# One soft-MoE kernel on one core: the first pair folded before it is turned, three expert matrices in other homes, and a new order of all steps

## The chip, the cores and the metric

One NeuronCore of a Trainium2 chip runs the whole program. The metric is device microseconds (us) of one execution; a lower time is better. TensorE does the matrix products and turns (transposes), VectorE and ScalarE the elementwise work and the copies out of PSUM, GpSimd a few elementwise steps, and SyncE (SP in the profile) issues every DMA from one queue, in order.

## The reference

The input x is (8, 2496, 256). It is transformed by a Fourier transform along the sequence and along the features, and the real part goes through a soft mixture of 8 experts with 4 slots each. Only the parts that matter:

```python
X = np.fft.fft(np.fft.fft(x, axis=1), axis=2).real     # 8 x 2496 x 256
x = X.reshape(19968, 256)
logits = x @ phi                                       # 19968 x 32
d = softmax over the tokens (axis 0) of logits
slot_input = d.T @ x                                   # 32 x 256
for e in range(8):                                     # 4 slots per expert
    h = np.maximum(slot_input[e] @ w1[e], 0.0)         # 256 -> 1024
    slot_out[e] = h @ w2[e]                            # 1024 -> 256
c = softmax over the slots (axis 1) of logits
return c @ slot_out                                    # 19968 x 256
```

The softmax over the tokens needs the maximum and the sum over all tokens, so no expert can start before all of x has been worked on, and no output before the experts are done.

## The kernel before, in words

The batch is worked on as four pairs (0 to 3). The 2496 tokens of a sequence are factored as 64 x 39, and each pair is loaded as five tiles `x{p}{t}` of 1 MB (tile 0 has 896 KB). A step is one short name in the string `PLAN`; the loop at the end of `_build` walks through it and issues each step's instructions to its engines. The order is written out by hand in this string: every engine gets its instructions in exactly this order, and waits only where it needs a result, a buffer or a transfer. `X020` loads half 0 of tile 2 of pair 0; `=x02:R0` says that the tile lives in home R0 from here on. A home is a fixed buffer: six R homes of 8 KB per partition, eighteen E homes of 4 KB, ten M, four D, two X homes, and eight B homes, the PSUM banks. A step that gives a home to a new tile waits until all readers of the old one are done. A suffix `/a` or `/v` says which engine copies, ScalarE or VectorE.

For each pair the steps are these. `F` adds a tile's rows to their mirror rows (VectorE, line 344), `G` and `H` add and subtract the halves of the feature axis and write the folded tile `e{p}{t}` into an E home (VectorE, line 355). `T` turns a folded tile on TensorE (line 360, four turns for each half), `A` copies the turned half out of PSUM, `Zo` and `Ze` multiply it by the folded phi (line 385), `Y`, `t`, `y`, `a`, `b`, `l`, `L`, `M` and `N` finish the logits. `R`, `V`, `v`, `vb`, `W` and `w` find the maxima, `E` takes exponentials, `q`, `e`, `f`, `d` and `D` bring them back to token order, and `u` multiplies them with the folded tiles `e{p}{t}` (line 595). An E home that held `e{p}{t}` is therefore free only after `u{p}{t}`. `sel`, `mm`, `mr`, `mx`, `me`, `ac`, `acT` (line 644), `at`, `si` and `sT` combine the pairs into the inputs of the slots.

Not all pairs go this way. In the kernel before, three tiles of pair 0 (0, 1 and 4) are turned raw: `TT` (line 370) turns the unfolded tile as soon as it has landed, adding the mirror row in PSUM, and `Zr` (line 417) folds the feature halves inside the product. The tiles are folded by `F`, `G` and `H` all the same, later, for step `u`. Pair 3 is loaded a second time, already turned (`XT`, `FT`, `Zt`), in both kernels.

The experts: w1 comes as eight matrices of 1 MB (`I0` to `I7`, tiles `w10` to `w17`, R homes), w2 as sixteen of 512 KB (`J0` to `J15`, E homes). `h` multiplies the slots by w1 (line 683), `r` is the ReLU on ScalarE, `x` a turn on VectorE, `s0j` and `s1j` multiply by w2 for the two halves of the output features (line 701, matrices J0 to J7 and J8 to J15). `so`, `rep` and `rh` spread the result.

The weights over the slots: `O` (line 721) and `Q` turn the logits back, `ca` to `ce` take the softmax over the slots (VectorE, ScalarE and GpSimd), `lT` and `lc` turn it. `po` is the last product (line 784), `ev` copies its four banks to an `o` tile in an R home, `S` stores it (line 796): halves of 512 KB for pair 0, whole tiles of 1 MB for the others. `dm` is a filler: a product of constants, whose result nobody reads (line 266).

Of the kernel before, what the change touches and what calls it, by code (L numbers as in the profile page):

```python
# [49 lines left out]
l00=bl00:B0,bm00:B2 y12/a=zt1:M4 F01 F12 H12=e12:E3 G12 X22=x22:R0 F22 H22=e22:E8 A110/a=et100:E9 A111/a  # L50
Zo10=bz10:B6 A100/a L010/a=lt0:M5 L011/a L000/a X20=x20:R1 F20 G22 T121=bT121:B1 T120=bT120:B4 Ze10 H20=e20:E4 G20
A121/a A120/a X21=x21:R4 F21 Y10/a Zo11=bz11:B3 Ze11 Y11/a t10=bt10:B5 M01 H21=e21:E5 y10/a T221=bT221:B1 N01
t11=bt11:B4 G21 y11/a T220=bT220:B6 X23=x23:R2 F23 G23=e23:E12 T201=bT201:B3 T200=bT200:B5 A201/a=et201:E10
X24=x24:R3 A220/a=et210:E14 XT34=xt34:R0 F24 H23 A200/a=et200:E9 a12=ba12:B4 b12/a=oo1:M6 a11=ba11:B3 b11/a
a10=ba10:B6 b10/a T211=bT211:B5 A221/a=et211:E17 A211/a T210=bT210:B4 A210/a l10=bl10:B7,bm10:B3 L101/a=lt1:M7
L001/a l11=bl11:B6,bm11:B1 Zo20=bz20:B5 Ze20 L100/a L110/a L111/a T230=bT230:B4 T231=bT231:B2 H24=e24:E16
T241=bT241:B3 Y20/a=zs2:M8 t20=bt20:B1 A231/a A241/a=et221:E10 G24 T240=bT240:B5 R01 V01=bv01:B2 A230/a y20/a=zt2:M9
Zo22=bz22:B3 A240/a=et220:E9 Zo21=bz21:B4 Ze22 Y22/a Ze21 Y21/a M10 M00 v01 FT34 Zt32=bz32:B1 XT33=xt33:R1
t22=bt22:B5 FT33 vb01/a=me01:X0 t21=bt21:B3 Y32/a=zs3:M0 XT32=xt32:R4 FT32 N00 N10 y21/a XT30=xt30:R2 W01
t32=bt32:B4 Zt31=bz31:B1 R00 V00=bv00:B0 y22/a a20=ba20:B3 a21=ba21:B5 y32/a=zt3:M1 w01/a E010=d01:D0 E011 R10  # L60
V10=bv10:B7 v00 Y31/a b20/a=oo2:M3 b21/a FT30 vb00/a=me00:X1 t31=bt31:B4 y31/a XT31=xt31:R3 a22=ba22:B2 W00 FT31
b22/a q011=q01:D1 M11 v10 vb10/a=me10:X0 J4=w24:E10 w00/v N11 q010 Zt30=bz30:B1 C3 l21=bl21:B3,bm21:B5
l20=bl20:B4,bm20:B2 E000=d00:D2 E001 R11 V11=bv11:B0 Y30/v t30=bt30:B6 q000=q00:D3 q001 L211/a=lt2:M2 L210/a M21 v11
vb11/v=me11:X1 W10 L201/a L200/a w10/a H01=e01:E17 M20 N20 C4 X30=x30:R0 J2=w22:E9 J11=w211:E14 X33=x33:R1
e01=be010:B1,be011:B5 y30/a E101=d10:D0 e00=be000:B2,be001:B7 f010/a=es0:M4 W11 w11/v G01 f011/v E100 R20
a30=ba30:B6 O02=bc02:B1 O00=bc00:B4 q101=q10:D2 Q00/v=c0:M6 a32=ba32:B0 a31=ba31:B5 N21 R21 q100 E110=d11:D1 f001/a
X34=x34:R4 X31=x31:R2 X32=x32:R3 f000/a d001=bd001:B7 d000=bd000:B2 b32/a=oo3:M8 b30/a b31/a l31=bl31:B0,bm31:B4
D001/a=ds0:M9 E111 q110=q11:D3 q111 D000/a L311/a=lt3:M3 L310/a l30=bl30:B6,bm30:B3 L300/a M31 N31
e10=be100:B5,be101:B7 L301/a f100/a=es1:M0 e11=be110:B2,be111:B4 M30 V21=bv21:B3 N30 f101/a v21 O20=bc20:B0 R31
Q20/a=c2:M1 vb21/a=me21:X0 f110/a f111/a V20=bv20:B5 v20 d101=bd101:B7 d011=bd011:B6 D011/a d100=bd100:B0  # L70
vb20/a=me20:X1 d010=bd010:B2 D100/a=ds1:M8 Q02/a V31=bv31:B4 I6=w16:R5 W21 D010/a w21/a O32=bc32:B6 E211=d21:D0 R30
W20 V30=bv30:B0 O01=bc01:B1 Q01/a F30 v31 vb31/v=me31:X0 u00=bu0:B2 v30 u01 F33 sel=bsel:B3 mm H33=e33:E7 u02 w20/a
E210 D101/a u03 q210=q21:D1 q211 u04 W31 vb30/a=me30:X1 E200=d20:D2 W30 O22=bc22:B1 O21=bc21:B5 O31=bc31:B3
O30=bc30:B7 U0/v w30/v w31/a E300=d30:D3 F32 mr G33 F34 Q22/a J10=w210:E17 J3=w23:E0 E201 q201=q20:D0 G32=e32:E2
d111=bd111:B2 d110=bd110:B4 Q30/a=c3:M4 D110/a e21=be210:B0,be211:B1 D111/a u10=bu1:B7 u11 u12 mx u13 u14 J5=w25:E11
H32 q200 f210/a=es2:M5 E301 f211/v E311=d31:D1 E310 Q32/a Q21/a me q301=q30:D2 e20=be200:B4,be201:B2 U1/a f200/a
f201/a I2=w12:R1 q300 I1=w11:R3 J6=w26:E13 e30=be300:B0,be301:B1 f301/a=es3:M2 f300/a G30=e30:E1 d211=bd211:B6
q311=q31:D3 q310 H30 e31=be310:B5,be311:B7 F31 ca00 G31=e31:E3 I4=w14:R0 f311/a f310/a d300=bd300:B4 d210=bd210:B2
D210/a=ds2:M0 Q31/a d201=bd201:B1 D300/a=ds3:M3 d301=bd301:B0 D301/a D211/v H31 ca20 d200=bd200:B7 J1=w21:E15 D200/a
# [816 lines left out]
```

## Time and profile before

| | us |
|---|---|
| median of 3 runs (174.19 to 175.49) | 174.72 |
| the profiled execution | 174.32 |
| its span, from the first to the last instruction | 172.5 |
| PE / DVE / ACT / POOL busy | 144.7 / 127.7 / 108.4 / 15.2 |
| moved by DMA | 64.34 MB: read 43.57, written 20.45 |

Times are of the profiled execution and count from the start of its span. What lies around the span is 1.8 us. A busy PE is not a PE at its peak, since the ends of matmuls are modelled and overlap the next one.

### The profile page before, as it was taken

What the parts mean: (1) busy time and instruction counts of PE and PEld (TensorE: products, weight loads), DVE (VectorE), ACT (ScalarE), POOL (GpSimd) and SP (SyncE); (2) the same over time, 40 slices, a digit from 0 to 9 for tenths busy, and PEclk for the clock granted to TensorE, in tenths of its full rate; (3) what the DMA queues carried; (4) which work ended last, traced back from release to release, by engine and by line L of the source; (5) the groups of instructions that cost most, each with busy time, mean ns of one, the idle gap of its engine ahead of it and who ended that gap; (6) DMA issues with size and microseconds to landing.
All of it is one profiled execution on the core that took longest, in us unless ns stands there. A gap on an engine that the chain in (4) does not pass through costs nothing.

```text
span 172.5 us, 5028 instructions
## 1 busy us (share of the span) xinstructions
PE 144.7 (84%) x2080; PEld 100.4 (58%) x2080; DVE 127.7 (74%) x226; ACT 108.4 (63%) x270; POOL 15.2 (9%) x27
## 2 busy tenths in 40 slices
PE   7298799999999999999999999699899988884000
...
DVE  0587979999999999899999789788966563066000
...
PEclk9879999999999999999999999999999999697555
...
GB/s 179 356 410 416 418 417 420 419 421 414 418 424 402 409 423 418 422 70 201 365 368 417 408 408 400 349 281 157 400 390 404 421 409 414 421 421 419 422 418 167
DMA packets 12406, 64.34 MB, mean 373 GB/s; under 512 B 1504, under 2 KB 1888, under 8 KB 7904
## 3 DMA queue, kind: packets, MB, share of 16 engines
...
q8 instruction: 16, 0.26, 0.6%
...
HBM read 43.57 MB, written 20.45 MB: 371 GB/s over the span
## 4 chain that ended last, share of the span: by engine, by line
PE 60%; DMA 19%; ACT 9%; issue 2%; SPq 1%; DVE 1%; ACTq 0%
PE B L784 10%; DMA R<-xh 6%; PE B L595 5%; DMA out<-R 5%; PE B L360 5%; PE B L569 5%; PE B L456 4%; PE B L385 4%; DMA R<-w1h 4%; DMA cs<-c 4%; PE B L701 4%; ACT M L260 4%; ACT R L260 3%; PE B L539 3%; PE B L402 3%; PE B L721 3%
## 5 line engine op out<-in xcount | busy, mean ns | idle before, releaser
L260 ACT COPY M<-B 128x480 f32<-128x480 f32 (+13 forms) x107 | 41.8, 441 | 8.6 <-PE B L385 2.1
L260 ACT COPY R<-B 128x512 f32<-128x512 f32 (+1 forms) x50 | 25.8, 590 | 10.8 <-PE B L784 5.8
L344 DVE TENSOR_TENSOR R<-R 128x1024 f32<-128x1024 f32 (+1 forms) x20 | 23.2, 1165 | 9.2 <-DMA R<-xh 9.1
L258 DVE COPY R<-B 128x512 f32<-128x512 f32 (+1 forms) x30 | 18.8, 664 | 14.4 <-PE B L784 12.2
L260 ACT COPY E<-B 128x512 f32<-128x512 f32 (+1 forms) x34 | 18.7, 596 | 16.0 <-PE B L360 8.0
L784 PE MATMUL B<-E,rh 32*128 32x512 f32 (+2 forms) x192 | 25.3, 577 | 3.6 <-ACT E L260 2.3
L355 DVE TENSOR_TENSOR E<-R 128x512 f32<-128x512 f32 x40 | 26.4, 686 | 0.6
L784 PEld LDWEIGHTS B<-E,rh 32*128 32x128 f32 x192 | 11.8, 200 | 11.2 <-ACT E L260 3.7
L760 POOL TENSOR_TENSOR M<-M,cm 128x640 f32<-128x640 f32 x8 | 10.0, 1263 | 83.9 <-DVE cm L755 83.9
L360 PE MATMUL B<-cs,E 128*128 128x128 f32 x96 | 13.9, 288 | 3.4 <-DVE E L355 3.4
L360 PEld LDWEIGHTS B<-cs,E 128*128 128x128 f32 x96 | 11.4, 147 | 5.0 <-DVE E L355 5.0
L526 ACT ACTIVATE D<-M,nm 124x128 f32<-124x128 f32 x44 | 14.2, 403 | 0.2
L266 PE MATMUL B<-warm 128*128 128x256 f32 x28 | 10.1, 476 | 1.1 <-POOL warm L821 1.1
L456 PE MATMUL B<-cs,M 128*128 128x128 f32 x88 | 10.8, 275 | 0.0
L456 PEld LDWEIGHTS B<-cs,M 128*128 128x128 f32 x88 | 10.4, 192 | 0.0
L569 PE MATMUL B<-M,cs 128*64 128x320 f32 x64 | 9.7, 439 | 0.4 <-issue 0.4
L595 PE MATMUL B<-E,M 128*32 128x129 f32 x320 | 9.5, 274 | 0.0
L385 PE MATMUL B<-E,wphi 128*32 128x256 f32 (+1 forms) x168 | 9.1, 352 | 0.0
L683 PE MATMUL B<-R,sT 128*32 128x512 f32 x64 | 7.7, 597 | 1.6 <-DMA R<-w1h 1.4
L595 PEld LDWEIGHTS B<-E,M 128*32 128x32 f32 x320 | 8.6, 110 | 0.8 <-ACT M L260 0.6
L701 PEld LDWEIGHTS B<-E,E 128*32 128x32 f32 x256 | 6.7, 110 | 3.3 <-issue 1.7
L491 DVE TENSOR_TENSOR M<-B,M 124x320 f32<-124x320 f32 (+1 forms) x16 | 8.0, 514 | 0.4 <-ACT M L260 0.3
(103 smaller groups left out, 199.3 us busy)
## 6 DMA issues: line engine op xcount, KB each, us to landing
...
```

The lines of the kernel that those rows point to most:

```text
L258: v.tensor_copy(dst, src)
L260: sc.copy(dst, src)
L344: v.tensor_tensor(x[:, lo], x[:, lo], x[:, hi], op=ALU.add)
L355: v.tensor_tensor(d, x[:, 0:4, 0:128], x[:, 0:4, 128:256], op=ALU.subtract if k else ALU.add)
L360: pe.transpose(b[:, g * 128 : g * 128 + 128], x[:, g, k * 128 : k * 128 + 128], ident)
L385: pe.matmul(z[32 * g : 32 * g + 32, o : o + n], wphi[:, w, :], turned_x(p, u, k)[:, g].rearrange("p h q a -> p (h q a)"), start=w != 0, st ...
L456: pe.matmul(d[:, i * 128 : i * 128 + 128], z[:, g].rearrange("p h q -> p (h q)"), C("wa"), start=True, stop=True)
L526: sc.activation(d[:, g], L[:, g], AF.Exp, bias=nms[:, p, hf, g : g + 1], scale=1.0)
L569: pe.matmul(b[64 * h : 64 * h + 64, :320], C("wb")[:, 64 * k : 64 * k + 64], s[:, 16 * hf : 16 * hf + 16, h], start=True, stop=True, tile_ ...
L595: pe.matmul(b[32 * g : 32 * g + 32, 0:129], d[:, k, c, :], x[:, c % 4, 0:129] if k == 0 else x[:, c % 4, 127:256], start=cc == 0, stop=cc ...
L701: pe.matmul(b[32 * g : 32 * g + 32], h[:, 4 * (2 * (j % 2) + f) + g, :], w[:, f, g], start=j == 0 and f == 0, stop=j == 7 and f == 1, tile ...
L784: pe.matmul(view(f"bp{p}{b}{i}", 512)[:, q * n : q * n + n], rh[rows, dc], l[rows, :n], start=True, stop=True, tile_position=(32 * i, 0),)
```

## The change

1. All five tiles of pair 0 are folded by VectorE first and then turned (`F`, `G`, `H`, `T`, `Zo`, `Ze`); no `TT` and no `Zr` is left.
2. `w17` comes in two halves of 512 KB in E homes (`I70` in E5, `I71` in E14), and `w214` and `w215` live in R homes (R0 and R3). The functions for it were there.
3. All steps stand in another order, with other homes; some copies change between ScalarE and VectorE. Pair 0's tiles are loaded in the order 3, 2, (pair 1's tile 0), 1, 0, 4 in place of 2, 3, (pair 1's tile 4), 0, 4, 1. The fillers are again fourteen: eight stand ahead of `acT` and six behind, before it was six and eight.
4. The table `wb`, equal to `wa`, is gone (64 KB less in `C2`), and `usb`, `sos` and the fillers' constants share one buffer, `spare`.

The diff, cut:

```diff
 PLAN = """
-dm4=bw4:B0 X021=x02:R0 dm13=bw13:B1 dm9=bw9:B2 dm3=bw3:B3 X020 F02 C0 X031=x03:R1 H02=e02:E0 T021=bT021:B4 G02 X030
-T020=bT020:B5 dm11=bw11:B6 A021/a=et011:E1 C1 F03 P phi=bphi:B7 H03=e03:E2 G03 T031=bT031:B0 X140=x14:R2 X001=x00:R3
-T030=bT030:B1 A020/a=et010:E3 X000 TT000=bT000:B2 wphi wneg A031/v Zo01=bz01:B3 A030/v Ze01 TT001=bT001:B4 X141
-A000/a=et000:E4 Y01/a=zs0:M0 F14 A001/a=et001:E5 H14=e14:E6 t01=bt01:B5 F00 G00=e00:E7 y01/a=zt0:M1 G14
-T141=bT141:B6 X040=x04:R4 X041 TT040=bT040:B7 TT041=bT041:B0 X011=x01:R5 T140=bT140:B1 A041/a=et021:E8 X010
-A040/v=et020:E9 TT010=bT010:B2 A010/a TT011=bT011:B3 A140/a=et120:E10 A011/a F04 H00 X10=x10:R0 Zr02=bz02:B4
-G04=e04:E11 A141/a=et121:E12 Zr00=bz00:B5 Zo12=bz12:B7 Y02/a Y00/a Ze12 Y12/a=zs1:M2 X13=x13:R1 t02=bt02:B0 y02/a
...
-u32 ac1 H34 ca31 cb00/v cb20/v cb01/v u24 U2/v u33 u34 ac2 ac3 dm12=bw12:B4 acT=bac:B0 at k0=bk0:B7 O10=bc10:B1
-si0=bs0:B5 cc20 I3=w13:R4 J9=w29:E4 J0=w20:E5 J8=w28:E1 cc00 sT0/a k2=bk2:B6 k3=bk3:B2 K3/a h100=bh10:B3 cc01 K2/a
-O12=bc12:B4 dm5=bw5:B0 I7=w17:R0 O11=bc11:B5 cd20 cd00 ca30 si1=bs1:B2 sT1/v k1=bk1:B6 K1/a K0/a h000=bh00:B0 h001
-h110=bh11:B2 h010=bh01:B6 h011 tk Q12/a=c1:M5 Q10/a cd01 ce01/g r00=hs00:D0 ca21 x00=hT00:E8 cb30/v I5=w15:R2
-s10=bo1:B7 s00=bo0:B4 s01 Q11/a h111 r01=hs01:D1 x01=hT01:E3 ca10 r11=hs11:D2 J7=w27:E12 h101 r10=hs10:D3 cb31/v
...
+dm1=bw1:B0 dm2=bw2:B1 dm13=bw13:B2 X031=x03:R0 X030 P F03 H03=e03:E0 X021=x02:R1 G03 C0 dm3=bw3:B3 T031=bT031:B4
+dm12=bw12:B5 X020 F02 A031/v=et011:E1 H02=e02:E2 T030=bT030:B6 C1 A030/a=et010:E3 phi=bphi:B7 X10=x10:R2
+T021=bT021:B0 A021/a G02 wphi X010=x01:R3 F10 H10=e10:E4 dm8=bw8:B1 G10 X011 F01 H01=e01:E5 X000=x00:R4
+T020=bT020:B2 Zo01=bz01:B3 A020/a T100=bT100:B5 dm4=bw4:B4 A100/a=et100:E6 Ze01 dm5=bw5:B6 Y01/a=zs0:M0 X001 F00
+H00=e00:E7 T011=bT011:B7 A011/a=et001:E8 t01=bt01:B1 X040=x04:R5 G01 X041 X12=x12:R0 G00 C2 X11=x11:R1 T001=bT001:B0
+T101=bT101:B2 T010=bT010:B4 y01/a=zt0:M1 A001/a F04 H04=e04:E9 X141=x14:R2 A010/a=et000:E10 T000=bT000:B5 A000/a
+Zo00=bz00:B6 G04 Ze00 Y00/a F12 T041=bT041:B3 T040=bT040:B7 H12=e12:E11 A041/a=et021:E12 t00=bt00:B1
+A040/a=et020:E13 y00/a Zo02=bz02:B0 Ze02 Y02/a T121=bT121:B4 wneg t02=bt02:B5 X140 G12 F11 H11=e11:E14
+A121/v=et111:E15 y02/a G11 T120=bT120:B6 a01=ba01:B3 b01/a=oo0:M2 F14 H14=e14:E16 A101/a=et101:E17 a02=ba02:B7 b02/a
+G14 a00=ba00:B1 b00/a T111=bT111:B0 A111/a X13=x13:R3 A120/a=et110:E1 T110=bT110:B5 l01=bl01:B4,bm01:B3
+L011/a=lt0:M3 A110/a L010/a l00=bl00:B2,bm00:B7 Zo10=bz10:B1 Ze10 T141=bT141:B0 T140=bT140:B6 F13 L001/a M01
+H13=e13:E3 Y10/a=zs1:M4 t10=bt10:B5 G13 T131=bT131:B3 A141/a=et121:E8 T130=bT130:B1 Zo12=bz12:B0 y10/a=zt1:M5 A131/a
...
+q201=q20:D0 q200 d010=bd010:B3 L301/a H31 M31 M30 N31 N30 E211=d21:D2 d011=bd011:B1 e20=be200:B4,be201:B7
+d101=bd101:B0 D010/a D011/a D001/a u00=bu0:B3 X32=x32:R0 u01 X34=x34:R1 R30 E110 u02 q111=q11:D3 q110 R31 k0=bk0:B1
+u03 u04 e11=be110:B2,be111:B5 E210 f200/a=es2:M2 f201/a U0/a f110/a F34 V30=bv30:B6 f111/a V31=bv31:B4 v30
+X33=x33:R2 v31 vb30/a=me30:X1 vb31/a=me31:X0 J0=w20:E7 I70=w170:E5 O12=bc12:B7 D101/a=ds1:M7 G34=e34:E2 q211=q21:D0
...
+J1=w21:E10 u30=bu3:B7 u22 u31 cc20 u23 H32=e32:E13 G32 u32 u24 u33 u34 U2/a O30=bc30:B1 Q30/a ca10 ac1 ac2 ac3
+acT=bac:B6 at si0=bs0:B2 k2=bk2:B0 cd20 si1=bs1:B5 sT0/a sT1/v ca30 K2/v ca31 I3=w13:R0 h000=bh00:B3 J11=w211:E9
+h100=bh10:B4 cd00 h001 J9=w29:E12 k3=bk3:B7 ce00/g I6=w16:R4 J6=w26:E17 h010=bh01:B1 h101 h011 cb21/g K3/a tk
+lT00=bl00x:B6 r00=hs00:D1 x00=hT00:E1 s00=bo0:B2 s01 J8=w28:E13 r01=hs01:D3 x01=hT01:E6 J15=w215:R3 J12=w212:E3
+h110=bh11:B5 r10=hs10:D2 x10=hT10:E2 h111 lc00/a=ls00:E7 cb30/g s02 cc30 r11=hs11:D0 s03 cd01 x11=hT11:E10 s04 s05
+ce01/v s06 cd30 cb10/g s07 cc21 so0/a lT01=bl01x:B0 rep0=br0:B7 cc10 rh0/a lc01/a=ls01:E5 ce20/g lT20=bl20x:B3
+po00=bp000:B1,bp001:B4,bp002:B6,bp003:B5 lc20/v=ls20:E14 ev001/v=o00:R2 po20=bp200:B2,bp201:B7,bp202:B0,bp203:B3
+ev000/a ev002/a ev003/v ev203/a=o20:R1 ev201/a s10=bo1:B1 s11 cd21 po02=bp020:B4,bp021:B6,bp022:B5,bp023:B3
...
-            ("wb", np.block([[np.cos(al), np.sin(al)], [-np.sin(al), np.cos(al)]])),
...
-        usb = const("usb", 128, NPAIR - 1, 129)
+
+        spare = const("spare", 128, (NPAIR - 1) * 129)
+        usb = spare.rearrange("p (i n) -> p i n", n=129)
...
-        sos = const("sos", 128, D)
+        sos = spare[:, :D]
...
-        warm = const("warm", 128, max(WARM)) if WARM else None
+        warm = spare[:, : max(WARM)] if WARM else None
...
-                    b[64 * h : 64 * h + 64, :320], C("wb")[:, 64 * k : 64 * k + 64], s[:, 16 * hf : 16 * hf + 16, h],
+                    b[64 * h : 64 * h + 64, :320], C("wa")[:, 64 * k : 64 * k + 64], s[:, 16 * hf : 16 * hf + 16, h],
```

## Rows read from the trace of the kernel before

**Rows 1.** The page's 40 equal slices of the span, and all that was moved.

```profile
PE   7298799999999999999999999699899988884000
DVE  0587979999999999899999789788966563066000
PEclk9879999999999999999999999999999999697555
GB/s 179 356 410 416 418 417 420 419 421 414 418 424 402 409 423 418 422 70 201 365 368 417 408 408 400 349 281 157 400 390 404 421 409 414 421 421 419 422 418 167
DMA packets 12406, 64.34 MB, mean 373 GB/s; under 512 B 1504, under 2 KB 1888, under 8 KB 7904
```

**Rows 2.** Five stretches: busy us of PE, PEld, DVE, ACT, POOL; clock, DMA, GB/s.

```profile
0.00:21.00 21.00, 14.52 (x129) 11.18 (x129) 12.81 (x22) 5.35 (x9) 1.44 (x15) 0.92 0.93 354
21.00:49.00 28.00, 28.00 (x349) 22.29 (x353) 26.39 (x36) 22.57 (x51) 0.24 (x2) 1.00 1.01 418
49.00:98.80 49.80, 49.35 (x955) 37.58 (x954) 48.10 (x92) 42.13 (x131) 0.00 (x0) 1.00 0.91 359
98.80:117.00 18.20, 16.58 (x314) 9.44 (x313) 14.98 (x33) 7.69 (x19) 7.32 (x5) 1.00 0.95 361
117.00:172.50 55.50, 36.29 (x348) 19.90 (x348) 25.41 (x47) 30.61 (x61) 6.20 (x5) 0.84 0.92 374
```

**Rows 3.** Waits of SP, the queue of all DMAs: total us, times, longest.

```profile
SPq L270 <- DVE E L355: 42.0, 18, 4.3
SPq L270 <- PE B L614: 11.8, 1, 11.8
```

**Rows 4.** The chain that ended last: start us, us, what.

```profile
22.97 2.74 PE B L417 x64
25.70 0.66 PE B L385 x24
...
27.16 0.87 PE B L360 x8
...
32.46 1.34 PE B L472 x16
...
103.96 7.09 DMA R<-w1h
...
148.87 8.32 DMA out<-R
```

**Rows 5.** Groups by line and shape: us busy, mean ns, idle before.

```profile
L355 DVE TENSOR_TENSOR E<-R 128x512 f32<-128x512 f32 x40 | 26.4, 686 | 0.6
L344 DVE TENSOR_TENSOR R<-R 128x1024 f32<-128x1024 f32 x16 | 19.4, 1219 | 8.2 <-DMA R<-xh 8.2
```

**Rows 6.** Timeline of PE at the start, and around the experts: start us, us.

```profile
7.94 1.97 PE L360 MATMUL B<-cs,E 128*128 128x128 f32 x8 [3.38 <-DVE E L355]
...
13.71 0.98 PE L370 MATMUL B<-cs,R 128*128 128x128 f32 x7 [1.06 <-DMA R<-xh]
14.63 1.50 PE L385 MATMUL B<-E,wphi 128*32 128x256 f32 x24
...
21.00 1.97 PE L370 MATMUL B<-cs,R 128*128 128x128 f32 x16 [0.89 <-DMA R<-xh]
...
101.31 0.54 PE L721 MATMUL B<-cs,M 124*128 124x124 f32 x3
101.69 0.60 PE L266 MATMUL B<-warm 128*128 128x256 f32 x2
102.12 0.59 PE L721 MATMUL B<-cs,M 124*128 124x124 f32 x4
...
111.09 1.06 PE L683 MATMUL B<-R,sT 128*32 128x512 f32 x8 [1.41 <-DMA R<-w1h]
...
116.91 1.14 PE L784 MATMUL B<-E,rh 32*128 32x512 f32 x8
```

**Rows 7.** Timeline of SP's queue: when the first store is issued.

```profile
119.59 41.71 SPq L796 DMA_DIRECT2D out<-R  x25
```

More of the change, by code (lines that the diff above doesn't have):

```diff
@@ L50 @@
[L50 to L79, printed above, removed]
@@ L85 @@
-s10=bo1:B7 s00=bo0:B4 s01 Q11/a h111 r01=hs01:D1 x01=hT01:E3 ca10 r11=hs11:D2 J7=w27:E12 h101 r10=hs10:D3 cb31/v
-cb21/g ce20/g x11=hT11:E2 x10=hT10:E16 ca11 cb11/v lT20=bl20x:B1 cb10/g cc10 cc30 ce00/g s02 s03 s04 s05
-lc20/v=ls20:E7 s06 s07 lT00=bl00x:B0 cc21 so0/a rep0=br0:B5 lT01=bl01x:B6 rh0/a lc01/a=ls01:E6 cd21 lc00/v=ls00:E1
-po20=bp200:B2,bp201:B3,bp202:B1,bp203:B4 ev203/v=o20:R3 ev200/a ev201/a cc31 cc11 ev202/v s11 s12 J13=w213:E5
-J15=w215:E15 J12=w212:E9 po00=bp000:B5,bp001:B6,bp002:B0,bp003:B2 ev000/a=o00:R5 ev001/a s13 cd10 cd30 s14 ev003/a
@@ new lines @@
+a21=ba21:B7 w00/v L111/a FT32 E001=d00:D0 M11 a22=ba22:B0 v10 N11 a20=ba20:B1 R11 V11=bv11:B3 E011=d01:D1
+vb10/a=me10:X0 W10 Y32/a=zs3:M1 b22/a=oo2:M2 t32=bt32:B5 b21/a b20/a l21=bl21:B6,bm21:B4 XT33=xt33:R5 C4 E000 FT33
+y32/a=zt3:M4 L211/a=lt2:M5 w10/a E010 l20=bl20:B0,bm20:B7 L210/a J7=w27:E15 XT31=xt31:R0 Zt31=bz31:B1 FT31
+q000=q00:D2 XT30=xt30:R1 FT30 Zt30=bz30:B5 v11 q001 M21 N21 vb11/v=me11:X1 e00=be000:B2,be001:B4 R21 V21=bv21:B6
+E100=d10:D3 L200/a L201/a M20 f000/v=es0:M7 N20 W11 Y31/a Y30/a O11=bc11:B7 t30=bt30:B1 E101 y30/a t31=bt31:B5
@@ new lines @@
+J5=w25:E8 O21=bc21:B2 O20=bc20:B0 w11/v O22=bc22:B3 y31/a v21 vb21/a=me21:X0 Q21/a=c2:M9 Q20/a Q11/a=c1:M0
+q011=q01:D0 R20 V20=bv20:B1 v20 vb20/a=me20:X1 q010 X31=x31:R2 q101=q10:D2 F31 q100 E111=d11:D1 a32=ba32:B5
+b32/a=oo3:M2 a31=ba31:B2 b31/a a30=ba30:B0 b30/a W20 W21 w20/v e01=be010:B7,be011:B5 l31=bl31:B2,bm31:B1 f001/a
+w21/v Q22/v E200=d20:D3 ca00 l30=bl30:B6,bm30:B0 X30=x30:R3 F30 G31=e31:E17 f010/a f011/a E201 e10=be100:B3,be101:B4
+I0=w10:R4 f100/a=es1:M3 f101/a L311/v=lt3:M1 d000=bd000:B7 I5=w15:R5 D000/a=ds0:M4 L300/a d001=bd001:B5 L310/v
@@ new lines @@
+S041 po30=bp300:B7,bp301:B6,bp302:B0,bp303:B1 ev302/a=o30:R1 ev300/a ev031/v ev301/a
+po32=bp320:B5,bp321:B4,bp322:B2,bp323:B3 ev303/v ce21/g lT22=bl22x:B1 dm0=bw0:B0 lT21=bl21x:B7 ev320/v=o32:R5
+ev323/a lc21/a=ls21:E13 S011 po11=bp110:B6,bp111:B5,bp112:B0,bp113:B3 ev113/a=o11:R4 S040 S031 ev111/a ev110/a
+lc22/v=ls22:E1 ev322/v dm11=bw11:B1 po33=bp330:B2,bp331:B7,bp332:B1,bp333:B3 ev331/a=o33:R0 ev333/a ev330/a cd11
+ev321/v ev112/v po24=bp240:B5,bp241:B4,bp242:B6,bp243:B0 ev332/v ce11/g lT12=bl12x:B7 S030 lc12/a=ls12:E12
```

54 lines of the change are left out of this document (30 added, 24 removed).

## The prediction

> **What bounds the kernel now.** I read the 40 slices first. Two things run through the whole span: the transfers, at 410 to 424 GB/s wherever they are not starved, and TensorE, at nine tenths or more from the fourth slice to the middle, with VectorE nearly as full [rows 1]. 64.34 MB at 420 GB/s are 153 us of a span of 172.5, so the transfers are starved for some 19 us: at the start, in slices 17 and 18 (70 and 201 GB/s), and between the last loads and the first stores (349, 281, 157). The stretches say what holds between these holes. From 21 to 98.8 us TensorE works 77.35 of 77.8 us; ahead of 21 us it waits 6.5 us, behind 98.8 us 1.6 us until the first product [rows 2]. VectorE idles 11.5 us of the same 98.8. After the first store is issued at 119.59 us [rows 7], 20.45 MB have to go out, 48.7 us at 420 GB/s, and the chain ends in such a store and what follows it [rows 4]. So the end is the time of the first stores plus a stretch that no order of steps shortens, and the time of the first stores is TensorE's work and waits ahead of the first product at 116.91 us [rows 6]. SP waits 11.8 us in one piece behind the sums for pair 3 [rows 3], which makes the hole in slices 17 and 18, but TensorE works through it: that hole costs nothing by itself.
>
> **Part 1, pair 0 by VectorE first.** Removed are 46 raw turns, 16 in 1.97 us, so 5.7 us, and two product groups Zr of 2.74 us together; added are 24 turns, 8 in 0.87, so 2.6, and two product groups Zo with Ze, 1.50 and 0.66 [rows 4, 6]. TensorE is relieved of 3.6 us. VectorE does no more than before, since every tile was folded anyhow, but TensorE now stands behind it. A raw turn started when its tile had landed: the last at 21.00 us; two of them waited for transfers, 1.06 and 0.89 us [rows 6]. Now F, H and G lie between, 1.22 + 0.69 + 0.69 us a tile [rows 5], against 2.5 us that a tile takes to land (1.05 MB at 418 GB/s). VectorE keeps that pace only just, and each copy that it also makes puts it behind. While TensorE waits for a fold, all its later steps are queued behind the turn, and ScalarE's copies wait for them.
>
> I follow it to a point at which both kernels have done nearly the same on TensorE. In the new order that is T131, the first turn of pair 1's tile 3, which waits for G13. Ahead of it VectorE works through tiles 1, 4 and 3 of pair 1. The bytes queued up to the end of tile 1 (X11) are 8.63 MB. Five slices (21.56 us) move 7.67 MB, so these are moved at 23.9 us [rows 1]. A tile is usable later than that: X010 closes 6.53 MB, moved at 18.8 us, and its turn starts at 21.00 [rows 6]. That lag of 0 to 2.2 us I take as 1.3, between the ends: 25.2 us. Three tiles at 2.5 us, a copy (A121, taken as long as one G, 0.7) and a small sum (M01, taken at 0.5) end at 33.9 us. The kernel before is at that time at the same place: from 21 us on TensorE has no wait [rows 2], and at 33.8 us it ends pair 0's l00 [rows 4], with all turns of pair 1 done but those of tile 2. The new order has then done the same with tile 3 in the place of tile 2, a large product group in the place of a small one (1.50 against 0.66), and one filler (0.60) that the old order has ahead of acT is done; but three turn groups O of pair 1 that stood behind acT (0.54 to 0.59 each, 1.7 together) are now ahead of it [rows 6]. What is left from 33.9 us to acT was 98.8 - 33.9 = 64.9 us, waits of 0.45 included; it becomes 64.9 - 0.8 - 0.6 + 1.7 = 65.2. **acT moves from 98.8 to 99.1 us, 0.3 later.** So the 3.6 us saved go into waits for the folds and into the earlier O groups. Bounds of this term: -1.0 to +1.2, by the lag.
>
> Would VectorE then become the bound? Ahead of 98.8 us it works 87.3 us [rows 2]; copies handed between it and ScalarE make that some 1 us more. By 33.9 us it has done nine tiles at 2.5 us and about 3 us of copies and small steps, so 25.5; 62.8 us remain in 65.2. It has 2.4 us to spare: close, but behind TensorE.
>
> **Part 2, the homes of the experts.** Before, two w1 matrices waited for the first products of the experts to free an R home; the last landed 7.09 us after its issue [rows 4], and TensorE waited 1.41 us for it [rows 6]. Now w17 sits in E homes and only I6 waits, for h000. It is needed at h110. From the start of h000 to there stand six w1 products, 1.06 us each alone [rows 6] and less in a row, the turn group lT00 and two groups s: some 6.8 us. I6 is issued when h000 ends, after 1.06. With the 7.09 us of the old one it lands 1.3 us late; with less queued ahead of it, down to the 2.5 us of its own bytes, it is in time. Between 0 and 1.3 I take 0.7, the rows giving no reason for either end. J15 and J14 wait for w1 products too, but serve the last two groups of s1, past the first product.
>
> **Part 3, the order from acT to the first product.** It took 18.2 us [rows 2]. The three O groups (1.7) and a filler (0.6) are gone from it [rows 6], and the wait of 1.41. 18.2 - 1.7 - 0.6 - 1.4 + 0.7 = 15.2. The first product starts at 99.1 + 15.2 = 114.3 us in place of 116.9, **2.6 us earlier**. The first store was a whole tile, issued 2.7 us after the product [rows 6, 7]; now it is a half, which needs one copy on each engine, some 0.9 us less. The following stores come as before, so I count half of that, **0.5 us**.
>
> **Part 4, the load queue.** Each load waits for the home of an earlier tile, and SP stands meanwhile: 42.0 us in 18 waits for folds [rows 3]. The new order has one critical place. X33 takes R2 from x31, which is free only after H31, and H31 stands late on VectorE: some 65 us of work by the mean durations, at 73 to 75 us with the idle time above. 28.9 MB are queued ahead of X33; the old run had moved 29.3 MB by 73.3 us [rows 1], so the queue runs dry at about 72.5. That gives a hole of 3 to 5 us in place of the old one (slices 17 and 18, 5.8 us), and behind X33 stand all of the experts' matrices but three. I6 closes 40.5 MB; from 76.5 us at 420 GB/s that is 104 us, and it is needed at 107: 3 us of further holes are free. Cost 0; without this cover, 1 us per us.
>
> **Part 5, the small things.** 64 KB less to load is 0.15 us of transfers in the hidden stretch. The shared buffer makes copies wait for fillers that are long done: 0; if it were not covered, a copy's length, 0.3. The fillers change place, not number; those in the store stretch lie beside transfers.
>
> **The sum** against the profiled execution: +0.3 - 2.3 - 1.4 + 0.7 - 0.5 = -3.2 (rounded terms), so 174.32 - 3.2 = 171.1. The median of the runs is 0.4 above the profiled execution: **171.5 us**. Bounds of the terms: lag -1.3 or +0.9, I6 -0.7 or +0.6, stores -0.4 or +0.5: 169.1 to 173.5.
>
> **Rivals.** *The gain is lost to VectorE or the load queue.* If VectorE idles as much as before (11.5 us, not some 9) with 1 us more to do, acT comes at about 100; if the holes of part 4 take 2 us more than are free, h110 waits 2 us. Together 2.7 us: 174.2, no change. For it: both kernels' queue waits mostly for folds; against it: VectorE's spare 2.4 us. 0.22.
>
> *TensorE's clock falls in the load stage, and it ends slower.* Place: T001 waits for G00, behind four fold steps, about 1.9 us with nothing to do; from there to the end of pair 0's products stand about 5 us of work. Price: after a wait of 3.38 us eight turns took 1.97 us, against 0.87 later [rows 4, 6]; the clock of 8 and 7 tenths in slices 1 and 2 says that part of it ran at 1.2 GHz, not 2.4 [rows 1]. So some 1 us is lost for each us of work that falls into the low level. If all 5 us run so and half of what follows them, 6 us are lost, minus 0.5 that VectorE leaves free: 177. It decides from 3.2 us lost. Against it: waits of 1.06 and 0.89 left the clock at full speed [rows 1, 6]. 0.12. The Trainium skill, "TensorE: Matmul & The Clock Gate", section "HAM oscillation — how this bites in real kernels", speaks against this change in the same way: a kernel whose TensorE work is cut into bursts by waits starts the next burst at the halved clock. By that rule the time is the 177 above; here the rows show the fall only after the longest of the waits.
>
> *Better than forecast:* waits for folds as small as those for tiles before and I6 in time: 169. 0.08. The forecast has 0.58.
>
> **How the numbers follow.** A measurement of this kernel tells about 1% (1.7 us) from no change. Below 173.0 lie most of the forecast (0.52) and the better case: 0.60. Within 1%: the rest of the forecast and most of the first rival: 0.26. Above 176.5: the clock, and the tail of the first rival: 0.14. The range takes in the bounds and the first rival: 169.1 to 176.0.
>
> **What would show it.** Right: no raw turns; TensorE waiting 1 to 2 us for G00 and again until about 34 us, and hardly from there to acT at about 99; the first product near 114; the first store near 116; slices between loads and stores fuller than 281 and 157. Wrong: acT after 101, a clock below full speed between 15 and 30 us, a hole in the loads beyond 6 us, or a wait of over 2 us at h110.

## The result, and the profile after

| | before | after |
|---|---|---|
| median of 19 runs each, taken together, us | 175.01 (173.56 to 176.22) | 173.19 (172.28 to 175.57) |
| the profiled execution, us | 174.32 | 173.97 |
| its span, us | 172.5 | 172.2 |

The ratio is 0.9908, 95% interval 0.9881 to 0.9934: the change makes the kernel 0.9% faster, 1.6 us, where 3.2 us had been forecast. The ratios here and below leave out executions that took over 1.5% longer than the fastest of their kernel. The two profiled executions differ by less than the medians: the one of after lies 0.8 us above its median, the one of before 0.7 us below. What differs from execution to execution is read below, in the experiments.

The page of the changed kernel, its 40 slices and all that was moved (they answer to [rows 1]):

```profile
PE   7299879999999999999999989599999999494000
DVE  0589799999999998999999785767778977253000
PEclk9999999999999999999999999999999999858555
GB/s 179 342 411 421 414 411 428 413 423 427 410 409 413 418 380 419 386 133 334 307 317 394 419 419 412 399 206 228 377 406 370 416 427 413 413 414 426 415 424 156
DMA packets 12550, 64.27 MB, mean 373 GB/s; under 512 B 1520, under 2 KB 1904, under 8 KB 8176
```

TensorE's row is as full as before to slice 25, and its granted clock reads 9 to slice 33. The deep hole in the loads is one slice long (133 in place of 70 and 201), but three slices of 307 to 334 GB/s follow it. Between loads and stores the slices read 206 and 228 in place of 281 and 157.

The same five stretches, busy us of PE, PEld, DVE, ACT and POOL, then clock, share of the DMA engines and GB/s (they answer to [rows 2]):

```profile
0.00:21.00 21.00, 15.50 (x124) 11.22 (x128) 12.67 (x19) 6.51 (x12) 1.26 (x13) 1.00 0.93 352
21.00:49.00 28.00, 27.05 (x336) 20.85 (x329) 27.39 (x40) 21.68 (x51) 0.48 (x4) 1.00 1.02 417
49.00:98.80 49.80, 49.80 (x960) 38.44 (x959) 47.97 (x93) 44.56 (x136) 0.00 (x0) 1.00 0.93 360
98.80:117.00 18.20, 15.71 (x272) 8.44 (x274) 12.38 (x30) 6.85 (x14) 6.81 (x6) 1.00 0.92 362
117.00:172.20 55.20, 37.15 (x362) 23.05 (x354) 28.58 (x51) 27.74 (x57) 6.85 (x6) 0.82 0.92 375
```

Up to 98.8 us TensorE works 92.35 us (15.50 + 27.05 + 49.80) in place of 91.87: the stage of the loads is as long as before. Behind it there is 2.5 us of idle time where there were 1.6.

TensorE's timeline around the experts, with idle time and releaser in brackets (it answers to [rows 6]):

```profile
99.17 0.32 PE L644 MATMUL B<-cs,acc 128*32 128x64 f32 x8
...
100.64 3.50 PE L683 MATMUL B<-R,sT 128*32 128x512 f32 x23
...
108.24 1.08 PE L701 MATMUL B<-E,E 128*32 128x128 f32 x32 [0.46 <-DVE E L693]
110.81 1.07 PE L683 MATMUL B<-R,sT 128*32 128x512 f32 x8 [1.49 <-DMA R<-w1h]
...
116.61 2.00 PE L784 MATMUL B<-E,rh 32*128 32x512 f32 x16
```

and the chain that ended last, in the same place (it answers to [rows 4]):

```profile
100.64 1.11 PE B L683 x8
101.75 0.02 issue
101.76 9.01 DMA R<-w1h
110.77 0.04 issue
110.81 1.92 PE B L683 x16
112.73 2.64 PE B L701 x96
```

acT stands at 99.17 us, and the first product h000 frees I6's home at 101.75. I6 is issued at once and lands 9.01 us later; h110 has waited 1.49 us for it. The first output product starts at 116.61 us, only 0.30 us before that of before [rows 6].

### The profile page after: what moved, and what is told of

It reads as the page before. It is cut to its first block, busy times and chain, and to the rows that moved or that the text cites. A ratio compares the mean times of both kernels' runs of the same rounds, so it can differ in the third digit from the quotient of the medians.

```text
span 172.2 us, 4950 instructions
## 1 busy us (share of the span) xinstructions
PE 145.2 (84%) x2042; PEld 102.0 (59%) x2042; DVE 129.0 (75%) x230; ACT 107.3 (62%) x265; POOL 15.4 (9%) x28
## 4 chain that ended last, share of the span: by engine, by line
PE 64%; DMA 22%; ACT 2%; SPq 1%; DVE 1%; issue 1%; ACTq 0%; DVEq 0%
DMA R<-xh 10%; PE B L784 9%; DMA out<-R 6%; PE B L456 6%; PE B L360 6%; PE B L569 6%; PE B L595 5%; DMA R<-w1h 5%; PE B L385 5%; PE B L701 4%; PE B L472 3%; PE B L721 3%; PE B L766 3%; PE B L539 3%; PE B L402 3%; PE B L436 2%
## 5 line engine op out<-in xcount | busy, mean ns | idle before, releaser
L260 ACT COPY M<-B 128x480 f32<-128x480 f32 (+14 forms) x105 | 41.6, 439 | 8.6 <-PE B L456 2.2
L784 PE MATMUL B<-E,rh 32*128 32x512 f32 (+2 forms) x192 | 26.6, 589 | 2.8 <-ACT R L260 2.5
L360 PE MATMUL B<-cs,E 128*128 128x128 f32 x120 | 18.1, 290 | 5.4 <-DMA cs<-c 3.4
L784 PEld LDWEIGHTS B<-E,rh 32*128 32x128 f32 x192 | 14.9, 196 | 9.4 <-ACT R L260 5.2
L360 PEld LDWEIGHTS B<-cs,E 128*128 128x128 f32 x120 | 14.3, 149 | 9.5 <-DVE E L355 8.6
L760 POOL TENSOR_TENSOR M<-M,cm 128x640 f32<-128x640 f32 x7 | 8.8, 1265 | 84.6 <-DVE cm L755 78.6
L266 PE MATMUL B<-spare 128*128 128x256 f32 x28 | 10.7, 495 | 1.1 <-POOL spare L821 1.1
L385 PE MATMUL B<-E,wphi 128*32 128x256 f32 (+1 forms) x216 | 11.4, 347 | 0.0
L266 PEld LDWEIGHTS B<-spare 128*128 128x128 f32 x28 | 5.8, 240 | 5.2 <-issue 1.7
L385 PEld LDWEIGHTS B<-E,wphi 128*32 128x32 f32 x216 | 5.8, 109 | 4.1 <-issue 1.4
```

The lines of the kernel that those rows point to most:

```text
L260: sc.copy(dst, src)
L266: pe.matmul(view(f"bw{i}", 512)[:, :n], warm[:, :128], warm[:, :n], start=True, stop=True)
L360: pe.transpose(b[:, g * 128 : g * 128 + 128], x[:, g, k * 128 : k * 128 + 128], ident)
L385: pe.matmul(z[32 * g : 32 * g + 32, o : o + n], wphi[:, w, :], turned_x(p, u, k)[:, g].rearrange("p h q a -> p (h q a)"), start=w != 0, st ...
L784: pe.matmul(view(f"bp{p}{b}{i}", 512)[:, q * n : q * n + n], rh[rows, dc], l[rows, :n], start=True, stop=True, tile_position=(32 * i, 0),)
```

## The experiments

The theory after the result, called **Q**: the load I6 lands late because of what stands ahead of it in the load queue, and this landing sets the first output product. The first rival, **V**: the chain on VectorE and ScalarE behind acT (k3, K3, tk, ReLU, turn) sets it, and the wait for I6 lies beside that.

**The changed kernel again, beside the next three.** No edit.

> The changed kernel once more, beside its variants. Both theories: 0.991 of the kernel before (some 1.6 us less). Theory Q (load queue): I6, the last w1 matrix, lands about 9 us after its issue because the queue ahead of it is full, and TensorE waits some 1.5 us for it at h110. Theory V (VectorE and ScalarE): what holds the first product is the chain k3, K3, tk, ReLU, turn, and the wait at h110 only covers it.

172.97 us (6 runs), ratio 0.9891 (0.9847 to 0.9934). In its profiled execution I6 landed at 110.94 us, h110 had waited 1.47 us, and the first product came at 116.78: the same chain.

**late_j: three J loads behind I6.**

```diff
-... I3=w13:R0 h000=bh00:B3 J11=w211:E9 h100=bh10:B4 cd00 h001 J9=w29:E12 k3=bk3:B7 ce00/g I6=w16:R4 J6=w26:E17 ...
+... I3=w13:R0 h000=bh00:B3 h100=bh10:B4 cd00 h001 k3=bk3:B7 ce00/g I6=w16:R4 J6=w26:E17 ...
-... s01 J8=w28:E13 r01=hs01:D3 ...
+... s01 J8=w28:E13 J9=w29:E12 J10=w210:E16 J11=w211:E9 r01=hs01:D3 ...
```

(J10 stood earlier, ahead of I1.)

> The changed kernel with J9, J10 and J11 (1.57 MB, needed only for s11 to s13) issued behind I6, J6 and J8. Theory Q: at 420 GB/s that is 3.7 us of queue, so I6 lands some 3.7 us earlier, near 107, h110 does not wait, the first product starts 1.5 us earlier, near 115.1, and the time is 1.5 us below the changed kernel's: 0.982 of the kernel before. Theory V: I6 lands earlier, but the first product moves by less than 0.5 us: 0.989 to 0.991.

172.16 us, ratio 0.9801 (0.9751 to 0.9851). The chain of late_j:

```profile
101.65 1.11 PE B L683 x8
102.76 0.02 issue
102.77 6.55 DMA R<-w1h
109.32 0.04 issue
109.36 1.92 PE B L683 x16
```

The load takes 6.55 us in place of 9.01, 2.5 us less and not the 3.7 expected; the wait at h110 is down from 1.49 to 0.25 us, and although acT came 1.0 us later in this execution (100.18), the first product came 1.4 us earlier, at 115.17. Q holds in its direction and in the time.

**early_tk: V's chain shortened.**

```diff
-... k2=bk2:B0 cd20 si1=bs1:B5 sT0/a sT1/v ca30 K2/v ca31 ... J9=w29:E12 k3=bk3:B7 ce00/g ... cb21/g K3/a tk lT00=bl00x:B6 ...
+... k2=bk2:B0 k3=bk3:B7 cd20 si1=bs1:B5 sT0/a sT1/v K2/v K3/a tk ca30 ca31 ... J9=w29:E12 ce00/g ... cb21/g lT00=bl00x:B6 ...
```

> The changed kernel with k3, K3 and tk moved ahead of the experts' products and of two maxima on VectorE. Theory Q: r00 and s00 come earlier by 0.5 us or more, but h110 still starts when I6 lands, near 110.8; first product within 0.2 us, time 0.991 of the kernel before. Theory V: first product 0.5 to 1.0 us earlier, 0.986 to 0.988.

173.57 us, ratio 0.9893 (0.9861 to 0.9925), the same as without the edit. tk ended at 102.48 us in place of 106.72, 4.2 us earlier, and the wait at h110 only grew to 1.59 us: whatever is done sooner waits for I6. In the profiled execution the first product came at 115.70, 0.9 us earlier than in that of after, which by itself is V's number; but I6 landed 0.9 us earlier too (109.85), and h110 again started 0.04 us behind it, so it is the landing that moved. V falls as the bound.

**both: the two edits together.**

> Both edits together. Theory Q: the chain shows only once the load is in time, so more than the two alone: first product 2.0 us earlier than in the changed kernel, 0.979 of the kernel before. Theory V: as early_tk alone, 0.986 to 0.988.

171.52 us, ratio 0.9792 (0.9752 to 0.9832), the best version together with both_h31 below; it beats both kernels, the one before by 3.5 us. Its interval covers the 0.9801 of late_j, so that the early tk adds to the late J loads is not shown. Its chain:

```profile
100.29 1.11 PE B L683 x8
101.40 0.02 issue
101.42 6.93 DMA R<-w1h
108.35 0.04 issue
108.39 1.92 PE B L683 x16
```

The wait at h110 is 0.44 us and the first product starts at 114.19 us: where the prediction had put it (114.3). From acT, which came at 98.82 us here, that is 15.4 us; in late_j it is 15.0, so behind acT the early tk brought nothing that this trace shows.

**late_i6: the opposite of late_j.** I6 stands behind J6 and J8 in the queue.

```diff
-... ce00/g I6=w16:R4 J6=w26:E17 h010=bh01:B1 ... s01 J8=w28:E13 r01=hs01:D3 ...
+... ce00/g J6=w26:E17 h010=bh01:B1 ... s01 J8=w28:E13 I6=w16:R4 r01=hs01:D3 ...
```

> The changed kernel, with the load I6 issued behind J6 and J8 (1.05 MB) where it stood ahead of them: the opposite of late_j. Theory Q (the bytes that stand ahead of I6 in the load queue set the first product): I6 lands about 2.5 us later (1.05 MB at 415 GB/s), near 113.3, the first product moves from 116.6 to about 119, and the ratio to before is about 1.005. Rival (I6's landing doesn't set the end, later work does): the ratio stays within 0.989 to 0.995.

177.39 us, ratio 1.0151 (1.0095 to 1.0207). Its profiled execution took 178.72 us, 1.3 more than the median, so it is read for the order of events and not for the size. Its page and three stretches of it (columns as above):

```profile
PEclk9999999999999999999999999659999999968555
```

```profile
100.00:109.00 9.00, 8.14 (x100) 3.07 (x92) 7.32 (x19) 2.85 (x7) 5.25 (x5) 1.00 1.02 410
109.00:113.00 4.00, 0.00 (x0) 0.00 (x0) 1.17 (x3) 0.49 (x1) 0.90 (x1) 0.87 0.70 285
113.00:122.00 9.00, 8.96 (x126) 5.70 (x130) 2.85 (x6) 2.84 (x6) 1.27 (x1) 0.68 0.33 96
```

and its timeline of TensorE:

```profile
113.04 1.93 PE L683 MATMUL B<-R,sT 128*32 128x512 f32 x8 [4.18 <-DMA R<-w1h]
...
116.45 3.94 PE L701 MATMUL B<-E,E 128*32 128x128 f32 x96
...
121.65 2.00 PE L784 MATMUL B<-E,rh 32*128 32x512 f32 x16
```

I6 landed at 113.00 us, 2.2 us later than in after: Q's number. But the first product came 5.0 us later, not 2.4: TensorE had nothing to do from 109 to 113 us, and what followed ran at a mean granted clock of 0.68, eight products in 1.93 us where after has 1.07, so the first of them at the lower level (1.2 GHz). From the landing of I6 to the first product it took 8.65 us, in after 5.84. So here the late load cost more than its lateness, behind a wait of 4.18 us; the 1.49 us of after did not do it (granted clock 1.00 from 98.8 to 117 us). By the ratios, late_i6 is 2.4% above after, 4.3 us against the 2.4 expected; that the clock is the whole of this excess is likely, but was seen in the one execution alone.

**before_j9: the kernel before, with J9 alone moved behind I7 and I5.**

```diff
-... si0=bs0:B5 cc20 I3=w13:R4 J9=w29:E4 J0=w20:E5 J8=w28:E1 ... I5=w15:R2 ... J7=w27:E12 h101 ...
+... si0=bs0:B5 cc20 I3=w13:R4 J0=w20:E5 J8=w28:E1 ... I5=w15:R2 ... J7=w27:E12 J9=w29:E4 h101 ...
```

> The kernel before, with one quarter-size load (J9, 0.52 MB) moved behind the I-loads I7 and I5 that the first product of the last stage waits for; nothing of the change is in it. Theory Q (the load queue's backlog sets the first product, in this kernel as in the changed one): I7 and I5 land about 1.2 us earlier (0.52 MB at 415 GB/s), the wait for I7's matrix at h101 falls from 1.41 us to at most 0.3 us, and the ratio to before is about 0.994. Rival T (TensorE's work ahead of the first product sets it): I5 lands earlier as well, but the ratio stays within 0.998 to 1.002.

174.03 us, ratio 0.9953 (0.9929 to 0.9977). I7 landed 1.6 us earlier than in before, at 106.97, but I5, for which h101 waits too, only 0.7 (110.36 in place of 111.05; 6.33 us after its issue in place of the 7.09 of [rows 4]), so the wait at h101 came down from 1.41 [rows 6] to 0.83 us and not to 0.3. The direction is Q's and T falls: half of the gain of the whole change is to be had by moving one load of 0.52 MB.

**early_h31: the fold that X33 waits for, two folds earlier.**

```diff
-... F30 G31=e31:E17 f010/a f011/a ... L301/a H31 M31 M30 N31 ...
+... F30 G31=e31:E17 H31 f010/a f011/a ... L301/a M31 M30 N31 ...
```

> The changed kernel, with VectorE's fold H31 taken two folds earlier, right behind G31, so that the load X33, which waits for it, is issued about 2.5 us earlier. Theory Q1 (the hole in the load queue at X33 is passed on to every load behind it): I6 lands 1.5 to 2.5 us earlier and the ratio to before falls to about 0.982. Theory Q2 (the loads behind X33 wait for folds and products of their own, so the hole only moves): I6 lands within 0.5 us of where it does now and the ratio stays near 0.990.

173.23 us, ratio 0.9914 (0.988 to 0.9949): no gain. X33 was issued 2.3 us earlier (72.45 in place of 74.78) and landed 2.4 us earlier, but the next load, J0, was issued at 77.15 in place of 77.12, since it waits for a step u of its own; I6 landed at 109.99, 0.8 us before that of after, between what the two theories expect and within what this landing varies by (109.83 to 110.94, see no_fillers). Q2 is nearer than Q1: the hole at X33 mostly moves. The edit has a price too: the sums q (line 531) that stood ahead of H31 on VectorE come later, and TensorE, 0.4 us ahead of after at 70 us, is 0.5 behind it from e11 (79 us) to acT.

**no_fillers: no dm12, dm8, dm4 and dm5.**

> The changed kernel without the four groups of filler products (dm12, dm8, dm4, dm5) that stand in its load stage; they compute nothing that is used. Clock theory (TensorE's clock stays full through the waits for folds only because the fillers keep it busy): the granted clock falls below full somewhere between 10 and 30 us and acT is ready at least 1 us later than 99.2. Rival (the work itself keeps the clock): the clock is full from 13 us on at the latest, acT is within 0.3 us of 99.2 and the time within 0.3 %.

173.04 us, ratio 0.9899 (0.9871 to 0.9928). The clock row of its page, and three lines of TensorE's timeline:

```profile
PEclk9999999999999999999999999999999999858555
```

```profile
12.04 1.97 PE L359 MATMUL B<-cs,E 128*128 128x128 f32 x8 [0.79 <-DVE E L354]
13.94 1.94 PE L384 MATMUL B<-E,wphi 128*32 128x256 f32 x16
...
19.16 1.97 PE L359 MATMUL B<-cs,E 128*128 128x128 f32 x16 [0.68 <-DVE E L354]
```

By the row the clock is as full as with the fillers, but the durations say otherwise at the start. The sixteen products at 13.94 us (line 384 here, 385 in after) take 1.94 us; in after they stand at 13.73 and take 1.07. So here TensorE ran at the lower level (1.2 GHz) until about 15.8 us, and in after, where four turns took 0.98 us at 11.95 and 0.60 at 13.20, until about 12.7. The traces' own records of the granted clock start at 16.02 us here and at 12.65 in after; the row shows as full what lies ahead of the first record. So the fillers do bring the full clock some 3 us earlier; once it is full, the work itself keeps it (sixteen turns in 1.97 us, as in after, behind a wait of 0.68 us and with no filler near). Neither theory came as it was written: the clock theory has the start right, but acT came at 99.86, 0.7 us later than in after and not 1; the rival has the time right (0.1% from after), but not the clock at 13 us and not acT.

Nor is this a test of less work. Line 266 has 6.7 us up to 98.8 us in after and 3.8 here, 2.9 us less, but the slower start took it back: TensorE was busy for 92.86 us up to acT, in after for 92.72. T131 came 0.4 us earlier, and the later acT is within what this step varies by from execution to execution (98.70 to 100.18 in orders that differ only behind it or in J loads). I6 landed at 109.83 and the first product came at 115.68, 0.9 us before the profiled execution of after with a later acT. So executions with the same loads in the same order differ by a microsecond in this landing, and the first product follows it.

**before_tile4 and before_tile4a: one tile of the change alone, in the kernel before.** Tile 4 of pair 0 is folded first; in the second version its eviction A040 stands on ScalarE, as in the changed kernel.

```diff
-... X041 TT040=bT040:B7 TT041=bT041:B0 X011=x01:R5 ... A041/a=et021:E8 X010 A040/v=et020:E9 ... F04 H00 ... Zr02=bz02:B4 G04=e04:E11 ... H04 ...
+... X041 F04 G04=e04:E11 H04 X011=x01:R5 ... A011/a T041=bT041:B0 T040=bT040:B7 A041/a=et021:E8 A040/v=et020:E9 H00 ... Zo02=bz02:B4 Ze02 ...
```

> The kernel before, with one part of the change alone and for one tile: the first pair's tile 4 is folded by VectorE and then turned, where it was turned raw and added up by products. It takes about 1.3 us of work from TensorE (four turned tiles fewer, and six products of 128 columns fewer), and adds nothing to VectorE but an earlier turn in its order. Theory Q (the load queue sets the first product): the gain is hidden by the wait for I7 and I5, ratio 0.997 to 1.001. Rival T (TensorE's work sets the end): the ratio is about 0.9925.

177.45 us, ratio 1.0129 (1.0078 to 1.018): both theories missed it. VectorE's timeline of before_tile4 shows why:

```profile
20.75 1.29 DVE L353 TENSOR_TENSOR E<-R 128x512 f32<-128x512 f32 x2
24.07 0.69 DVE L256 COPY E<-B 128x512 f32<-128x512 f32 x1 [2.03 <-PE B L358]
24.68 0.68 DVE L353 TENSOR_TENSOR E<-R 128x512 f32<-128x512 f32 x1
```

The copy A040 now waits 2.03 us for the turn T040, which stands behind a raw turn that waits for its own tile; the folds of the next tiles are queued behind the copy. G13 ended at 29.42 in place of 27.61, T131 started 1.55 us later, acT 1.1 us, and the last two w1 loads landed 2.2 us later.

> As before_tile4 (the kernel before, with the first pair's tile 4 folded first), but with the eviction A040 on ScalarE, where the changed kernel has it, and not on VectorE. Theory W (in before_tile4 VectorE stood 2.03 us in front of A040 for its product, with the folds of the next unit queued behind): that wait is gone, T131 comes back from 30.1 to within 0.6 us of the 28.5 of before, and the ratio is 0.996 to 1.003. Rival (folding the tile early makes VectorE late in any case): T131 stays at 29.6 or later and the ratio is 1.008 or more.

175.75 us, ratio 1.007 (1.0033 to 1.0108). With the copy on the other engine the wait is gone, T131 starts at 28.88 us and acT at 98.62: theory W holds for the place. The time doesn't follow wholly. The profiled execution is the fastest of its twelve, with the span of before (172.5 us), so it doesn't show where the others lose 1.2 us; that stays open. It does show what became of TensorE's work: it was busy 0.7 us less up to acT (91.14 in place of 91.85), but waited 1.38 us for a fold at 19.08 us, where before has no such wait. So the fold ahead of the turn took back most of what it saved.

**both_h31: all three edits.**

> The changed kernel with the late J loads, the early turn step tk and the early fold H31 together. Theory Q: the loads behind X33 come up to 0.9 us earlier, as they did with the fold alone; of that the wait of 0.44 us at h110 can be taken back, so the first product comes up to 0.5 us earlier than with the first two alone and the ratio is 0.976 to 0.979. Rival (with the wait at h110 this small TensorE's own work is the bound): the ratio stays near 0.979 to 0.981.

171.84 us, ratio 0.9867 (0.9828 to 0.9905), outside the ranges of both theories; its median is 0.3 us above that of both, whose runs were taken on another chip, where before had 175.04 and not 174.45. I6 landed at 107.41, 1.0 us before h110, and its chain has no load in it any more:

```profile
105.21 0.29 DVE cm L755
...
105.64 1.28 POOL M L760
...
106.96 0.66 PE B L766 x4
107.61 1.01 PE B L701 x32
108.63 1.72 PE B L683 x16
```

The first product starts at 114.22 us, as in both (114.19), though acT came 0.7 us later (99.49 in place of 98.82). So the rival is nearer: nothing is gained by the earlier load, and in this execution the bound has passed from the load to the softmax over the slots on VectorE and GpSimd (lT00 waits for it) and TensorE's own work. Whether the later acT is a price of the early H31 (0.5 us in early_h31) or chance is not shown.

**before_again: a second profiled execution of the kernel before.**

> The kernel before, unchanged, for a second profiled execution, since the two profiled executions differ by less than the medians do. If the first product sets the end in each execution, this one has the last store landing 52.0 us behind the issue of its first store, as in the first profile (119.59 to 171.59), within 0.3 us, and the time differs from 174.3 only as the landing of I5 differs from 111.05. Otherwise the executions differ in the stage of the stores, and the stretch from first store to last landing is longer by over 0.3 us.

174.6 us. From the issue of the first store to the landing of the last it took 51.99 us (119.85 to 171.84), before 52.00; I5 landed 0.26 us later than in the first profile and the end came 0.25 later. The two profiles of the changed kernel have 52.74 and 52.72 us there. So executions differ ahead of the first store, and the store stage of a kernel is a constant. The fourteen profiled executions together say it of the whole way. From the landing of the last w1 matrix that had to wait for a home (I5, I6) to the first product it takes 5.84 to 5.87 us in twelve of them; the other two are late_i6, with its lower clock (8.65), and both_h31, where the load is in time (6.81). From the first product to the last landing it takes 54.4 to 54.9 us in all fourteen. This is the second half of Q: the landing sets the first product, and the first product sets the end.

## Why the prediction was wrong

**Part 1 was right in its sum, but by another way: its closeness is in part luck.** acT was forecast at 99.1 us and came at 99.17; T131 at 33.9 and came at 34.77. T131 does not wait for G13, as the prediction reads it: it turns the half that H13 writes. H13 ended at 34.27 us, and G13 at 34.87, 1.0 us later than forecast, when T131 was already running; TensorE came to T131 from its own work. And the 3.6 us saved did not become waits for folds. TensorE's waits for folds in the load stage, by its timeline:

```profile
15.03 0.66 PE L360 MATMUL B<-cs,E 128*128 128x128 f32 x4 [0.23 <-DVE E L355]
...
18.86 1.97 PE L360 MATMUL B<-cs,E 128*128 128x128 f32 x16 [0.68 <-DVE E L355]
...
23.21 1.26 PE L360 MATMUL B<-cs,E 128*128 128x128 f32 x8 [0.95 <-DVE E L355]
```

These are 1.9 us in all, where the raw turns of before had waited 1.06 and 0.89 us for their tiles [rows 6], and from 23.21 us to acT there is none. By groups of lines up to 98.8 us, the raw turns and Zr are gone (5.8 and 3.3 us), the turns cost 4.2 us more (18.1 against 13.9) and Zo with Ze 2.3 more (11.4 against 9.1): 2.6 us saved, not 3.6. The O groups cost the 1.7 of the forecast more (6.1 against 4.4) and the fillers 1.5 (6.7 against 5.2). So the saving was spent on work that had stood elsewhere. Whether less work on TensorE would bring acT nearer was not shown: no_fillers left it as busy, and in before_tile4a new waits took most of it back (acT at 98.62 us; before has 98.78 and, in its second profile, 99.37).

**The failing step is the term for I6, in part 2, and the cover that part 4 gave it.** The term was taken at 0.7 us, with bounds of 0 to 1.3: I6 lands 6.4 us after its issue, at most the 7.09 us of the old load [rows 4]. It took 9.01. The lower bound had no ground either: X33, issued at 74.78 us in after with nothing but the end of X34 ahead of it, landed 5.03 us later, and not the 2.5 us of its bytes. h110 was forecast 7.5 us after the start of h000 and came 10.17 after it. From acT to the first product it took 17.44 us where 15.2 had been summed up: 2.2 us of the 3.2 are lost here. "I6 closes 40.5 MB; from 76.5 us at 420 GB/s that is 104 us" fails twice. Two windows of the trace of after that end at 104 us and at the landing:

```profile
76.50:104.00 27.50, 26.95 (x605) 19.62 (x609) 25.84 (x53) 18.62 (x58) 0.00 (x0) 1.00 0.97 365
104.00:110.77 6.77, 4.87 (x64) 2.07 (x56) 4.95 (x12) 3.23 (x6) 6.15 (x5) 1.00 1.02 408
```

At 365 GB/s and not 420, 1.3 MB were missing at 104 us (39.2 MB had been moved), so that the 40.5 MB were moved at 107.4: 3.4 us late, which the 3 us called free would nearly have covered; the loads behind X33 wait one by one for the readers of their homes, which is the row of 334, 307 and 317. (Four of the experts' matrices stand ahead of X33, J7, J5, I0 and I5, and not three as part 4 says.) And at the landing not 40.5 but 41.9 MB had been moved: the first of I6's sixteen shares landed at 106.82 us, the last at 110.77, and the first of J6's, issued behind it, at 108.11. That is the other 3.4 us. It was in part in the rows of before: I5 was also issued into a full queue and landed 7.09 us later, while its own 1.05 MB are 2.5 us. The first share of I5 came 4.82 us after its issue, that of I6 5.06: against the old load it is the lag between the shares that grew, from 2.27 to 3.95 us. What spreads the shares no run shows; it varies between executions, 2.68 to 3.95 us in the four named below.

I6 was not alone in being late. I3, issued at 96.55 us, landed at 105.74, and h011 waited for it, as TensorE's weight loads (PEld) show; beside them no gap between products shows, since the ends of products are modelled:

```profile
105.78 0.15 PEld L683 LDWEIGHTS B<-R,sT 128*32 128x32 f32 x7 [0.35 <-DMA R<-w1h]
```

The six products from h000 on took 6.5 us (100.64 to 107.13), and 5.4 in early_tk and both, where I3 landed at 104.89 and 103.11.

The Trainium skill, "DMA: Bandwidth & Descriptors", section "Why a DMA increments its semaphore by 16 and not by 1", says that a transfer is spread over up to sixteen engines and that only all sixteen completions together mean that the data is there. The trace agrees: the wait at h110 ended with the share that came 3.95 us after the first.

**The term for the stores, 0.5 us, was worth nothing.** The first store came 2.0 us after the first product and not 2.7 (118.57 - 116.61; before 119.59 - 116.91), much as forecast, but the stretch from the first store on grew from 52.0 to 52.7 us. From first product to last landing it is 54.68 us before (171.59 - 116.91) and 54.70 after (171.31 - 116.61). The first rows go out earlier after the first product, the same number of bytes ends no earlier. The slices between loads and stores, which were to be fuller, read 206 and 228 in place of 281 and 157: together the same.

With these, the sum closes: -3.2 + 0.1 (acT) + 2.2 (I6) + 0.5 (stores) = -0.4 us, and the two profiled executions differ by 0.35. The medians differ by 1.8. The landing of I6 differs between executions, 109.83 to 110.94 in four of them (after, after_again, early_tk, no_fillers) that have the same loads ahead of it, and that of I5 came at 111.05 and 111.31; that this makes up the rest is likely, but the executions at the medians have no trace. Which part of the change brings the 1.6 us isn't shown either: the fold of one tile was tried alone and gained nothing (before_tile4a), the homes and the order were not tried apart.

**The rivals.** The first, by its load-queue half, is what happened: h110 waited, though 1.49 us and not over 2, because the steps from h000 to there had taken 8.7 us (100.64 to 109.32, the end of s01) and not 6.8. Its VectorE half did not: VectorE worked 88.02 us up to 98.8, 0.7 more than before. The clock rival didn't come about in its place: the waits of 0.68 and 0.95 us left the granted clock at 1.00 (stretches above), and the sixteen turns behind the first of them took 1.97 us, full speed by the durations too, also without fillers (no_fillers, 19.16 us). The rule of the Trainium skill, "TensorE: Matmul & The Clock Gate", section "HAM oscillation — how this bites in real kernels", named in the prediction, is borne out elsewhere: in late_i6 the burst behind the wait of 4.18 us ran at a granted clock of 0.68 on average. None of the signs that the prediction named for being wrong came (acT after 101 us, the clock, a hole beyond 6 us, over 2 us at h110), and yet h110 came late: a wait reads short when the steps ahead of it are late as well.
